# A routed feed-forward kernel: tokens' split forms made one product at a time in a group's last step

## Chip, core and metric

One core of a Trainium2 chip runs the whole program in one launch. The metric is the device time of one execution in microseconds (us); the time before is the median of three runs.

## What is computed

Three stages follow each other: an attention through 32 packed vectors, a dense feed-forward with silu, and a soft mixture of 8 experts with relu. The change lies in the last stage.

```python
def _moe2_ref(x, w_gate, w1, w2):            # x: 2304 x 512, w1: 8 x 512 x 1024, w2: 8 x 1024 x 512
    logits = x @ w_gate
    P = np.exp(logits - logits.max())
    for _ in range(8):
        P /= P.sum(1, keepdims=True) + 1e-09
        P /= P.sum(0, keepdims=True) + 1e-09
        P *= N / E
    for e in range(E):
        h = np.maximum(x @ w1[e], 0.0)
        out += P[:, e:e + 1] * (h @ w2[e])
```

## The kernel before, in words

Every float32 product is made of three matmuls: an operand x is stored as hi (a rounded copy, cast on ACT, line 113) and lo (x - hi, a subtraction on DVE, line 114). The helper `split` issues this pair; such a pair is called a split form below.

The last stage takes the tokens in three groups of two blocks of 384 (`GRP`, line 610), and for each group 16 steps: 8 experts by two halves of the hidden width (`steps`, line 611). A step s multiplies the tokens' 512 channels by a 512 x 512 piece of w1 (`up`, line 822) and, one step later, the hidden values by a piece of w2 (`down` in group 0, `down7` in groups 1 and 2, line 956). Steps 0 to 15 are group 0, 16 to 31 group 1, 32 to 47 group 2.

`up` uses a seven-product scheme on 2 x 2 blocks (two halves of the channels by two blocks of tokens). Its products are numbered 1 to 7 and always run in the order `ORD = [1, 2, 6, 7, 5, 3, 4]` (line 613). Product p multiplies a form of the weights, `wf[s, p]`, by a form of the tokens, `xf[g, c, p]`; c counts the two 128-channel pieces of a half. The token forms of a group are the blocks b11, b21, b22 and four differences: t1 = b12 - b11, t2 = b22 - t1, t3 = b22 - b12, t4 = b21 - t2. They are made once a group and read in all its 16 steps:

```python
        w = wf[s, p]
        for c in range(2):
            x = xf[g, c, p]
            for l, r in ((0, 0), (0, 1), (1, 0)):
                pe.matmul(ps, w[:, l, c, 128 * i:128 * i + 128], x[:, r], ...)
```

`x_forms` (line 747) makes them: first all seven of c = 0, then all seven of c = 1, each a tile [128, 2, 384] in a pool `xf` of 14 slots. So a slot of the next group's form comes free only when the last step of the group has run the product that reads the old one. For group 0 the source is the tokens in SBUF (`pre_forms`, run between the dense stage's tiles); for groups 1 and 2 it is blocks loaded from DRAM by `x_load` (line 1142), 192 KB each, into slots of the pool `cp`, where the differences (`x_tmp`) and the copies of PSUM results in `up` (line 844) also live. That pool has `CP = 10` slots.

The steps are issued by the loop at line 1180. In each step it calls `up` for both row halves i of product n, then a `down` piece, and in between takes a step from a list of background generators (`bg`): loads or forms of the next step's weights, loads of the w2 forms, and last, in a group's last step, `x_forms` of the next group. The list is worked off in order, so what is left of it, `x_forms` above all, is issued by the `while gens` loop after the step's last product.

The order on each engine is not written by hand here: a scheduler turns the calls into one instruction stream per engine, by priority and free slots. All loads and stores go through SP's queue, in order. In groups 1 and 2 the accumulators in PSUM are seeded by ACT (line 969, `d <- M`), and ACT or DVE brings the sums back (lines 981, 983).

## Time and profile before

| what | value |
|---|---|
| median of 3 runs | 1872.11 us (1869.1 to 1873.45) |
| profiled execution, its own time | 1873.27 us |
| its span in the trace | 1871.3 us |
| PE busy | 1835.2 us (98%) |
| DVE busy | 1320.3 us (71%) |
| ACT busy | 931.4 us (50%) |
| attention and dense stage | 0 to about 402 us |
| group 0, 1, 2 | from 401.9, 895.4 and 1370.3 us |

The page cuts the span into 40 slices; PE shows 9 (90% or more) in nearly all of them, with one 8 in slice 30, where the granted clock also shows 8. The start of a group is the start of the first matmul of its first step on PE. Stretches that are named by two times are read from the start of the span.

### The profile page before, as it was taken

The page shows a single profiled execution, that of the slowest core. Times are in us where ns is not written, and L with a number is a line of the kernel's source. Part 1 is how long each engine was busy: PE and PEld are TensorE (multiplying, and loading weights), DVE is VectorE, ACT ScalarE, POOL GpSimd, SP SyncE. Part 2 cuts the span into 40 slices and gives each one's busy share as a digit, 9 for nine tenths or more (in the row PEclk, how much of TensorE's full clock was granted, in tenths as well). Part 3 has the DMA queues.
Part 4 walks back from the last instruction along what each step waited for, and adds up shares of the span by engine and source line. Part 5 has one row for each costly group of instructions (what it writes and reads, how often), then busy time and mean ns, then how long its engine had stood idle before and what let it go on. Part 6 is the DMA issues. An engine that isn't in the chain of part 4 may idle for free.

```text
span 1871.3 us, 28617 instructions
## 1 busy us (share of the span) xinstructions
PE 1835.2 (98%) x10715; PEld 1728.1 (92%) x10715; DVE 1320.3 (71%) x2251; ACT 931.4 (50%) x1842; POOL 2.8 (0%) x10
## 2 busy tenths in 40 slices
PE   6999999999999999999999999999989999999998
PEld 4898999998898989898899999999979999999998
DVE  6877654669987878786666667666677667666676
ACT  5776443444454444443354454545554454444544
POOL 0000000000000000000000000000000000000000
PEclk9999999999999999999999999999989999999999
DMA  9233100088898888887788888888878888888882
GB/s 347 98 90 92 57 13 1 33 294 308 309 335 308 301 304 302 304 306 263 268 259 248 264 259 258 261 251 263 259 226 279 268 259 258 262 247 263 261 255 93
DMA packets 168697, 436.34 MB, mean 233 GB/s; under 512 B 15456, under 2 KB 63216, under 8 KB 168560
## 3 DMA queue, kind: packets, MB, share of 16 engines
q1 hardware_dynamic: 168560, 434.52, 70.4%
q8 instruction: 85, 1.39, 0.3%
q14 instruction: 52, 0.43, 0.1%
HBM read 309.08 MB, written 125.38 MB: 232 GB/s over the span
## 4 chain that ended last, share of the span: by engine, by line
PE 91%; DMA 4%; DVE 2%; ACT 1%; issue 1%; SPq 0%; DVEq 0%; ACTq 0%
PE d L973 25%; PE X L837 21%; PE m L880 13%; PE Z L837 10%; PE g L548 9%; PE Y L837 5%; PE g L514 5%; PE u L490 1%; DMA xr<-x2d 1%; DMA q<-in_qT_dram 1%; DMA rawin<-in_moe_w_in_dram 1%; PE pp L321 0%; PE s L349 0%; PE lg L999 0%; DMA rawout<-in_moe_w_out_dram 0%
## 5 line engine op out<-in xcount | busy, mean ns | idle before, releaser
L973 PE MATMUL d<-hi,w2l 128*128 128x384 f32 x1792 | 495.8, 336 | 0.0
L114 DVE TENSOR_TENSOR lo<-hb,hi 128x768 fp32r<-128x768 f32 x224 | 213.8, 955 | 273.9 <-PE d L973 212.8
L973 PEld LDWEIGHTS d<-hi,w2l 128*128 128x128 f32 x1792 | 327.9, 188 | 6.5 <-ACT d L969 6.5
L973 PE MATMUL d<-lo,w2l 128*128 128x384 f32 x896 | 299.9, 335 | 0.0
L837 PE MATMUL X<-xf,w1l 128*128 128x384 f32 x1536 | 289.3, 336 | 6.3 <-ACT xf L113 5.9
L880 PE MATMUL m<-w2t,h 128*128 128x512 f32 x1152 | 280.4, 393 | 1.2 <-DVE cp L848 1.2
L837 PEld LDWEIGHTS X<-xf,w1l 128*128 128x128 f32 x1536 | 269.2, 189 | 7.9 <-ACT xf L113 6.8
L880 PEld LDWEIGHTS m<-w2t,h 128*128 128x128 f32 x1152 | 214.5, 188 | 43.0 <-DVE cp L848 1.5
L981 ACT COPY M<-d 128x384 f32<-128x384 f32 x232 | 111.7, 481 | 223.7 <-PE d L973 223.7
L113 ACT CAST hi<-hb 128x768 fp32r<-128x768 f32 x224 | 184.0, 836 | 56.6 <-DVE hb L934 30.2
L844 ACT COPY cp<-X 128x384 f32<-128x384 f32 x224 | 107.5, 480 | 207.0 <-PE X L837 207.0
L548 PE MATMUL g<-gT,woh 128*128 128x288 f32 x1024 | 205.7, 296 | 0.0
L548 PEld LDWEIGHTS g<-gT,woh 128*128 128x128 f32 x1024 | 163.6, 188 | 10.5 <-DVE gT L522 6.5
L973 PEld LDWEIGHTS d<-lo,w2l 128*128 128x128 f32 x896 | 168.6, 188 | 0.0
L548 PE MATMUL g<-gT,wol 128*128 128x288 f32 x512 | 150.5, 294 | 0.0
L837 PE MATMUL Z<-xf,w1l 128*128 128x384 f32 x768 | 145.7, 337 | 4.2 <-ACT xf L113 4.2
L837 PE MATMUL X<-xf,wf 128*128 128x384 f32 x768 | 146.7, 338 | 1.8 <-ACT cp L844 1.7
L837 PEld LDWEIGHTS X<-xf,wf 128*128 128x128 f32 x768 | 135.8, 188 | 8.4 <-ACT cp L844 2.9
L837 PEld LDWEIGHTS Z<-xf,w1l 128*128 128x128 f32 x768 | 135.0, 189 | 4.9 <-ACT xf L113 4.5
L983 DVE TENSOR_TENSOR M<-d,M 128x384 f32<-128x384 f32 x204 | 112.3, 551 | 11.7 <-PE d L973 11.6
L969 ACT COPY d<-M 128x384 f32<-128x384 f32 x216 | 104.5, 484 | 18.1 <-DVE hb L810 14.7
L514 PE MATMUL g<-a2h,U 128*128 128x288 f32 x512 | 108.9, 297 | 0.7 <-ACT U L494 0.6
(178 smaller groups left out, 2380.2 us busy)
## 6 DMA issues: line engine op xcount, KB each, us to landing
w1l<-w1d SPq DMA_DIRECT2D x224, 512.0 KB, 4.7
w2l<-w2d SPq DMA_DIRECT2D x224, 512.0 KB, 4.4
w1d<-wf SPq DMA_DIRECT2D x112, 512.0 KB, 5.2
r<-in_moe_w_dram SPq DMA_DIRECT2D x64, 512.0 KB, 5.9
w2d<-T SPq DMA_DIRECT2D x64, 512.0 KB, 4.2
w2d<-w2t SPq DMA_DIRECT2D x96, 256.0 KB, 3.4
rawin<-in_moe_w_in_dram SPq DMA_DIRECT2D x16, 512.0 KB, 4.6
rawout<-in_moe_w_out_dram SPq DMA_DIRECT2D x16, 512.0 KB, 5.5
```

Of the source, the lines that this page charges most:

```text
L113: act.copy(out=hi, in_=raw)
L114: eng.tensor_tensor(out=lo, in0=raw, in1=hi.bitcast(F32), op=ALU.subtract)
L490: pe.matmul(ps[64 * j:64 * j + 64, :w], ppT[b, g][:, 64 * j:64 * j + 64], win[c, k // per][:, k % per, :], start=True, stop=True)
L514: pe.matmul(ps[:, :HS], lhs, rhs, start=(n == 0), stop=(n == 5))
L548: pe.matmul(ps[:, :HS], lhs, rhs, start=(n == 0), stop=(n == 3 * nf - 1))
L837: pe.matmul(ps, w[:, l, c, 128 * i:128 * i + 128], x[:, r], start=(n == 0 and p in ((1, 7) if g else (1, 2, 7))), stop=(n == 5), skip_grou ...
L844: act.copy(out=t, in_=ps)
L880: pe.matmul(ps, h[:, l, 128 * tt:128 * tt + 128], w[:, r], start=(n == 0), stop=(n == 11))
L969: act.copy(out=ps, in_=m)
L973: pe.matmul(ps, w[:, l, c, 128 * d:128 * d + 128], r[:, c], start=(n == 0 and not seed), stop=(n == 5), skip_group_check=seed)
L981: act.copy(out=m, in_=ps)
L983: dve.tensor_tensor(m, ps, m, op=ALU.add)
```

## The change

`x_forms` now works in the order of the products: at each call it makes one form for both channel pieces, in one tile [128, 2, 2, 384], and `xf` is a pool of 7 such slots. For groups 1 and 2 a block of tokens is loaded with both pieces in one transfer of 384 KB into a pool `xr` of 4 slots, which opens when the last step of group 0 begins (where `r1`, the raw w1 pool, is closed). Each cast and each subtraction covers 128 x 768 elements. Differences are written over the block that is no longer read; b22 is overwritten by t2 and loaded a second time for form 3. The generator is no longer in the background list: in a group's last step it is called once after product n, for n from 1 to 6, so that form ORD[n-1] is issued when the product that reads the old one has been issued, and a seventh time after the last. `CP` falls from 10 to 6.

```diff
--- before.py
+++ after.py
@@ -24,7 +24,7 @@
 BLK = 384
 FH = 512
 EPS = 1e-9
-CP = 10
+CP = 6
 
 WID = [512, 512, 512, 512]
 
@@ -744,40 +744,42 @@
         form(3, s4)
         yield
 
-    def x_forms(g, src, tmp):
-
-        for c in range(2):
-            b11, b12, b21, b22 = src(c, 0), src(c, 1), src(2 + c, 0), src(2 + c, 1)
-
-            def form(p, x):
-                t = st["xf"].tile([128, 2, BLK], F32R, tag="xf", name=f"xf{g}{c}{p}")
-                split(t[:, 0], t[:, 1], x)
-                xf[g, c, p] = t
-
-            form(1, b11)
+    def x_forms(g, src, new):
+
+
+        b11, b21, b12, b22 = src(0, 0), src(1, 0), src(0, 1), src(1, 1)
+
+        def less(n, old, a, b):
+            t = new(n, old)
+            for o, x, y in zip(t, a, b):
+                dve.tensor_tensor(o, x, y, op=ALU.subtract)
+            return t
+
+        def form(p, x):
+            t = xf[g, p]
+            for c, y in enumerate(x):
+                c = slice(None) if len(x) == 1 else c
+                split(t[:, 0, c], t[:, 1, c], y)
+
+        def place(p):
+            xf[g, p] = st["xf"].tile([128, 2, 2, BLK], F32R, tag="xf", name=f"xf{g}{p}")
+
+        for n, p in enumerate(ORD):
+            place(p)
+            if p == 6:
+                t1 = less(1, b11, b12, b11)
+                t3 = less(3, b12, b22, b12)
+                t2 = less(2, b22, b22, t1)
+                b22 = src(1, 1)
+                form(6, t2)
+            elif p == 4:
+                form(4, less(4, b21, b21, t2))
+            else:
+                form(p, b11 if p == 1 else b21 if p == 2 else t3 if p == 7 else t1 if p == 5 else b22)
             yield
-            form(2, b21)
-            yield
-            t1, t2 = tmp(g, c, 1), tmp(g, c, 2)
-            dve.tensor_tensor(t1, b12, b11, op=ALU.subtract)
-            dve.tensor_tensor(t2, b22, t1, op=ALU.subtract)
-            form(6, t2)
-            yield
-            t3 = tmp(g, c, 3)
-            dve.tensor_tensor(t3, b22, b12, op=ALU.subtract)
-            form(7, t3)
-            yield
-            form(5, t1)
-            yield
-            form(3, b22)
-            yield
-            t4 = tmp(g, c, 4)
-            dve.tensor_tensor(t4, b21, t2, op=ALU.subtract)
-            form(4, t4)
-            yield
 
     def open_early():
-        st["xf"], s_ = pool("xf", 14, side="right", reuse_waits="tile"); ctx.enter_context(s_)
+        st["xf"], s_ = pool("xf", 7, side="right", reuse_waits="tile"); ctx.enter_context(s_)
         st["r1"], st["r1_st"] = pool("r1", 2, side="right", reuse_waits="tile")
         load_w1(0, 0)
         load_w1(0, 1)
@@ -794,9 +796,13 @@
 
         def src(k, h):
             q = GRP[0][h]
-            return x2[q // 3][k][:, BLK * (q % 3):BLK * (q % 3) + BLK]
-
-        yield from x_forms(0, src, lambda *k: pair(*k)[:, :BLK])
+            return [x2[q // 3][2 * k + c][:, BLK * (q % 3):BLK * (q % 3) + BLK] for c in range(2)]
+
+        def new(n, old):
+            t = unit([128, 2, 512], F32, f"tmpx{n}")
+            return [t[:, c, :BLK] for c in range(2)]
+
+        yield from x_forms(0, src, new)
         yield from w1_forms(0, lambda s, n: pair("w", s, n).rearrange("p (c f) -> p c f", c=2))
 
     X, Y, Z, cp = {}, {}, {}, {}
@@ -832,9 +838,9 @@
         w = wf[s, p]
         n = 0
         for c in range(2):
-            x = xf[g, c, p]
+            x = xf[g, p]
             for l, r in ((0, 0), (0, 1), (1, 0)):
-                pe.matmul(ps, w[:, l, c, 128 * i:128 * i + 128], x[:, r],
+                pe.matmul(ps, w[:, l, c, 128 * i:128 * i + 128], x[:, r, c],
                           start=(n == 0 and p in ((1, 7) if g else (1, 2, 7))), stop=(n == 5),
                           skip_group_check=p in (2, 6, 5, 3, 4))
                 n += 1
@@ -1140,13 +1146,10 @@
         return st["S"].tile([128, 2, 256], F32, tag="S", name=f"S{s}{n}")
 
     def x_load(g, k, h):
-        t = st["cp"].tile([128, BLK], F32, tag="cp", name=f"xr{g}{k}{h}")
+        t = st["xr"].tile([128, 2, BLK], F32, tag="xr", name=f"xr{g}{k}{h}")
         q = GRP[g][h]
-        nc.sync.dma_start(t, x2d[k, :, BLK * q:BLK * q + BLK])
-        return t
-
-    def x_tmp(g, c, n):
-        return st["cp"].tile([128, BLK], F32, tag="cp", name=f"xt{g}{c}{n}")
+        nc.sync.dma_start(t, x2d[2 * k:2 * k + 2, :, BLK * q:BLK * q + BLK].rearrange("k p n -> p k n"))
+        return [t]
 
     load_w2(0, 0)
     load_w2(0, 1)
@@ -1170,7 +1173,6 @@
     def later_pools():
         while old:
             old.pop().close()
-        st["r1_st"].close()
         for name, n, side in (("pb", 2, "left"), ("hb", 6, "left"), ("M", 8, "left"), ("hi", 5, "left"),
                               ("lo", 4, "left")):
             st[name], s_ = pool(name + "2", n, side=side, reuse_waits="tile")
@@ -1188,7 +1190,12 @@
             gens.append(w2_loads(s))
         last_of_group = s < NS and s + 1 < NS and steps[s + 1][0] != steps[s][0]
         if last_of_group:
-            gens.append(x_forms(steps[s + 1][0], lambda k, h: x_load(steps[s + 1][0], k, h), x_tmp))
+            if s + 1 == G0:
+                st["r1_st"].close()
+                st["xr"], s_ = pool("xr", 4, side="right", reuse_waits="tile")
+                ctx.enter_context(s_)
+            xform = x_forms(steps[s + 1][0], lambda k, h: x_load(steps[s + 1][0], k, h),
+                            lambda n, old: old)
         hform = h_forms(s - 1) if s > G0 else iter(())
         next(hform, None)
         for n, p in enumerate(ORD):
@@ -1197,6 +1204,8 @@
                     up(s, i, p)
                     pump_sk()
                     bg()
+                if last_of_group and n:
+                    next(xform)
             if s > G0:
                 next(hform, None)
                 down7(s - 1, DORD[n])
@@ -1214,6 +1223,8 @@
                 bg()
         if G0 <= s < NS and s % 2 == 0:
             load_pb(steps[s][0], steps[s][1] + 1)
+        if last_of_group:
+            next(xform)
         while gens and s < NS:
             bg()
```

What this makes of the streams, at three places. In names, X32, Y32, Z32 are the PSUM tiles of step 32 (a last digit for i), d30 and d31 those of `down7` for steps 30 and 31, xf2cp (before, as xf201: group 2, c = 0, p = 1) and xf2p (now) the token forms, xr the loaded blocks.

PE, where group 2 begins, before:

```order
L837 MATMUL X320_14583<-xf201_14513,w1l32_1_14223 128x384 x3
L837 MATMUL X321_14594<-xf201_14513,w1l32_1_14223 128x384 x3
L837 MATMUL Z320_14707<-xf207_14528,w1l32_7_14305 128x384
L837 MATMUL Z321_14714<-xf207_14528,w1l32_7_14305 128x384
L837 MATMUL Z320_14707<-xf207_14528,w1l32_7_14305 128x384 x2
L837 MATMUL Z321_14714<-xf207_14528,w1l32_7_14305 128x384 x2
L837 MATMUL X320_14583<-xf211_14550,w1l32_1_14223 128x384
L837 MATMUL X321_14594<-xf211_14550,w1l32_1_14223 128x384
L837 MATMUL X320_14583<-xf211_14550,w1l32_1_14223 128x384 x2
L837 MATMUL X321_14594<-xf211_14550,w1l32_1_14223 128x384 x2
L837 MATMUL Y320_14584<-xf202_14516,w1l32_2_14255 128x384 x2
```

PE, the same place now, from the last matmuls of step 31:

```order
L979 MATMUL d3041_14477<-hi30_4_14425,w2l30_4_14165 128x384
L843 MATMUL X320_14501<-xf21_14239,w1l32_1_14180 128x384 x6
L843 MATMUL X321_14512<-xf21_14239,w1l32_1_14180 128x384 x6
L843 MATMUL Y320_14502<-xf22_14283,w1l32_2_14212 128x384 x3
L979 MATMUL d3111_14534<-hi31_1_14497,w2l31_1_14402 128x384
L979 MATMUL d3111_14534<-lo31_1_14498,w2l31_1_14402 128x384
L979 MATMUL d3111_14534<-hi31_1_14497,w2l31_1_14402 128x384
L979 MATMUL d3110_14525<-hi31_1_14497,w2l31_1_14402 128x384
```

Before, products 1 and 7 of the first channel piece stand between those of the second; now product 1 is whole, and `d31` follows after half of product 2.

ACT, the end of step 31, before:

```order
L113 CAST hi31_7_14645<-hb3101_14428 128x768
L113 CAST hi31_5_14684<-hb3100_14263 128x768
L113 CAST xf202_14516<-xr220_14509 128x384
L981 COPY M14_10329<-d3040_14480 128x384
L113 CAST xf206_14523<-xt202_14520 128x384
L113 CAST xf207_14528<-xt203_14526 128x384
L113 CAST xf205_14531<-xt201_14519 128x384
L113 CAST xf203_14534<-xr221_14511 128x384
L113 CAST xf204_14539<-xt204_14537 128x384
L113 CAST xf211_14550<-xr210_14542 128x384
L113 CAST xf212_14553<-xr230_14546 128x384
L113 CAST hi31_6_14724<-hb3111_14385 128x768
```

ACT now, from product 5 of step 31 to the copies of step 32's first product:

```order
L113 CAST xf25_14421<-xr200_14231 128x768
L987 COPY M16_10209<-d3060_14385 128x384
L975 COPY d3020_14429<-M12_10250 128x384
L113 CAST hi31_3_14521<-hb3111_14364 128x768
L113 CAST xf23_14465<-xr211_14329 128x768
L975 COPY d3040_14468<-M14_10286 128x384
L987 COPY M12_10250<-d3020_14429 128x384
L113 CAST hi31_7_14563<-hb3101_14410 128x768
L113 CAST xf24_14487<-xr210_14233 128x768
L987 COPY M14_10286<-d3040_14468 128x384
L113 CAST hi31_5_14602<-hb3100_14220 128x768
L857 COPY Y320_14502<-X320_14501 128x384
```

Before, thirteen of the fourteen casts of group 2's forms stand behind the cast hi31_5, and the last five of them even behind the copies into Y32; now the seven casts stand in step 31, each between seeds (L975) and copies (L987) of `down7`.

SP, in step 31, before:

```order
L1145 DMA xr200_14505<-x2d_111 128x384
L648 DMA w2l31_6_14499<-w2d15_6_9689 128x1024
L1145 DMA xr201_14507<-x2d_111 128x384
L648 DMA w2l31_2_14501<-w2d15_2_9653 128x1024
L1145 DMA xr220_14509<-x2d_111 128x384
L648 DMA w2l31_4_14503<-w2d15_4_9655 128x1024
L1145 DMA xr221_14511<-x2d_111 128x384
L648 DMA w1l33_1_14592<-w1d1_1_4673 128x1024
L648 DMA w1l33_2_14624<-w1d1_2_4687 128x1024
L915 DMA pb21_14881<-pd_110 128x3x128 x2
L1145 DMA xr210_14542<-x2d_111 128x384
```

SP now, where group 1 begins (there is one more load of group 2's tokens, the second of b22, in step 31 behind the second of its w2 loads):

```order
L1151 DMA xr200_14231<-x2d_111 128x2x384
L921 DMA pb10_9892<-pd_110 128x3x128 x2
L921 DMA pb11_10005<-pd_110 128x3x128 x2
L716 DMA w2d15_2_9678<-w2t1510_9675 256x1x256
L716 DMA w2d15_4_9680<-w2t1510_9675 256x1x256
L1151 DMA xr210_14233<-x2d_111 128x2x384
L716 DMA w2d15_2_9678<-w2t1511_9692 256x1x256
L716 DMA w2d15_4_9680<-w2t1511_9692 256x1x256
L1151 DMA xr201_14235<-x2d_111 128x2x384
```

Before, the tokens of group 2 were loaded in step 31 behind the w2 forms; now four of five loads stand at the start of group 1.

## Rows read from the trace of the kernel before

**Rows 1.** Page, part 1: busy time, share of the span and instructions of each engine.

```profile
PE 1835.2 (98%) x10715; PEld 1728.1 (92%) x10715; DVE 1320.3 (71%) x2251; ACT 931.4 (50%) x1842; POOL 2.8 (0%) x10
```

**Rows 2.** Chain in order of time, whole span: start us, us, what.

```profile
882.67 6.48 DMA xr<-x2d
...
1373.36 8.02 DMA xr<-x2d
```

**Rows 3.** Timeline of PE, 868:930: start us, us, engine, line, op; idle before in brackets.

```profile
895.43 0.68 PE L837 MATMUL X<-xf,w1l 128*128 128x384 f32 x3
898.27 1.16 PE L837 MATMUL X<-xf,w1l 128*128 128x384 f32 x5 [2.15 <-ACT xf L113]
899.26 1.20 PE L837 MATMUL Z<-xf,w1l 128*128 128x384 f32 x4
900.88 1.65 PE L837 MATMUL X<-xf,w1l 128*128 128x384 f32 x4 [0.41 <-DVE xf L114]
902.32 0.53 PE L837 MATMUL Z<-xf,w1l 128*128 128x384 f32 x1
902.64 16.67 PE L880 MATMUL m<-w2t,h 128*128 128x512 f32 x72
```

**Rows 4.** Timeline of PE, 1352:1400: the last product of step 31, and step 32.

```profile
1366.12 2.24 PE L837 MATMUL Z<-xf,w1l 128*128 128x384 f32 x12
1368.20 0.33 PE L973 MATMUL d<-hi,w2l 128*128 128x384 f32 x1
...
1370.28 1.21 PE L837 MATMUL X<-xf,w1l 128*128 128x384 f32 x6
1375.67 2.51 PE L837 MATMUL Z<-xf,w1l 128*128 128x384 f32 x6 [4.19 <-ACT xf L113]
1381.97 2.29 PE L837 MATMUL X<-xf,w1l 128*128 128x384 f32 x6 [3.78 <-ACT xf L113]
1384.23 1.01 PE L837 MATMUL Y<-xf,w1l 128*128 128x384 f32 x2
...
1387.99 0.34 PE L973 MATMUL d<-lo,w2l 128*128 128x384 f32 x1
```

**Rows 5.** Groups by shape: busy us, mean ns of one, and idle before.

```profile
L114 DVE TENSOR_TENSOR lo<-hb,hi 128x768 fp32r<-128x768 f32 x224 | 213.8, 955 | 273.9 <-PE d L973 212.8 <-ACT d L969 55.7 <-ACT hi L113 5.3
...
L113 ACT CAST hi<-hb 128x768 fp32r<-128x768 f32 x224 | 184.0, 836 | 56.6 <-DVE hb L934 30.2 <-PE d L973 14.1 <-DVE hb L810 7.6
...
L114 DVE TENSOR_TENSOR xf<-xt,xf 128x384 fp32r<-128x384 f32 x16 | 8.2, 550 | 0.3 <-ACT xf L113 0.2
...
L113 ACT CAST xf<-xt 128x384 fp32r<-128x384 f32 x16 | 7.5, 512 | 4.9 <-DVE xt L763 4.9
```

**Rows 6.** Windows: length, busy PE, PEld, DVE, ACT, POOL (x), PEclk, DMA share, GB/s.

```profile
864.25:895.40 31.15, 31.15 (x157) 28.13 (x156) 20.84 (x37) 13.61 (x28) 0.00 (x0) 1.00 0.82 276
1341.10:1370.28 29.18, 29.18 (x170) 28.95 (x168) 17.95 (x28) 14.63 (x28) 0.00 (x0) 1.00 0.85 275
1370.30:1384.20 13.90, 5.92 (x19) 4.20 (x17) 10.19 (x21) 5.22 (x11) 0.00 (x0) 0.63 0.55 164
402.00:500.00 98.00, 93.54 (x482) 83.49 (x482) 92.22 (x212) 51.97 (x101) 0.00 (x0) 1.00 0.88 315
500.00:531.00 31.00, 31.00 (x157) 27.99 (x156) 28.59 (x51) 15.66 (x31) 0.00 (x0) 1.00 0.91 330
```

**Rows 7.** DMA issues of the whole span: KB each, median us to landing.

```profile
w2l<-w2d SPq DMA_DIRECT2D x224, 512.0 KB, 4.4
...
xr<-x2d SPq DMA_DIRECT2D x16, 192.0 KB, 6.0
```

**Rows 8.** Timeline of SP's DMA queue, 1325:1392: issues of w2 forms in step 31.

```profile
1353.83 6.56 SPq L648 DMA_DIRECT2D w2l<-w2d  x4
```

**Rows 9.** Timeline of ACT, 1340:1390: a form's cast and the seed behind it.

```profile
1365.64 0.51 ACT L113 CAST xf<-xr 128x384 fp32r<-128x384 f32 x1 [3.01 <-DMA xr<-x2d]
1366.06 0.48 ACT L969 COPY d<-M 128x384 f32<-128x384 f32 x1
```

## The prediction

> **What bounds the kernel now.** I read the page's busy times first: PE is busy 1835.2 us of the span, DVE and ACT far less [rows 1]. So only time in which PE waits, or runs slowly, can be won: some 36 us in all. Next I read the chain that ended last, in order of time: between long stretches of matmuls it has a few transfers, and late in the program only loads of token blocks (`xr`), two before each of groups 1 and 2; one of each pair stands here [rows 2]. Then I read PE's timeline around those two places.
>
> Where group 1 begins, PE starts seventeen matmuls of 384 columns between 895.43 and 902.64, waiting twice for token forms [rows 3]. Undisturbed, twelve of them take 2.08 us (1366.12 to 1368.20), 0.173 each [rows 4]. Seventeen would take 2.95, so 7.21 - 2.95 = **4.26 us** are lost.
>
> Where group 2 begins, eighteen such matmuls stand between 1370.28 and 1384.23, with waits of 4.19 and 3.78 us for ACT's casts [rows 4]: 13.95 - 3.12 = **10.83 us**. In this stretch the granted clock averages 0.63, so part of it is spent at the lower level (1.2 GHz instead of 2.4) [rows 6]. The twelve matmuls that follow, from 1384.23 to 1387.99, take 3.76 instead of 2.08 [rows 4]: **1.68 us** more. Together 16.77 us.
>
> The cause is the order of issue. The next group's forms are issued behind everything else of a group's last step, and the second set of loads needs `cp` slots that the first set and its differences hold.
>
> **The change, part by part.**
>
> *Forms between the products.* Product 1 of a new group needs form 1 alone, whose slot comes free when the last step has run product 1, more than 20 us earlier. Form 4, the last, is needed six products into the new group. In PE's new order product 1 of step 32 follows d30_4 with no other form in between. All three lost pieces should go: -16.77 us, the lowered clock with them, since it fell only after PE had waited.
>
> *What the forms cost where they now stand.* Per group ACT gets seven casts of 128 x 768. The same shape takes 0.836 us [rows 5]: 5.9 us, against 14 x 0.512 = 7.2 before. DVE gets seven subtractions for lo, 0.955 each by the same shape [rows 5], and four for the differences; for those I take 0.955 too: 11 x 0.955 = 10.5 us, against 22 x 0.55 = 12.1 before. It is less work, but all of it now falls into the last step. Step 15 (864.25 to 895.40) has DVE busy 20.84 of 31.15 us, of which 8 x 0.55 are already early form work; with 10.5 it becomes 26.9, or 87%. Step 31 (1341.10 to 1370.28) has 17.95 of 29.18, one subtraction of it form work; it becomes 27.9, or 96% [rows 6].
>
> Does PE lose time with DVE so full? Two stretches bound it [rows 6]. From 500 to 531 DVE is busy 28.59 of 31.00 (92%) and PE loses nothing. From 402 to 500 it is busy 92.22 of 98.00 (94%) and PE lacks 4.46 us, 1.4 per 31. So step 15 costs 0 and step 31 between 0 and 1.4; nothing in these steps can be won, since PE is never idle there. I take the middle, 0.7, because DVE's own lateness needs a step to reach PE and step 32 has room again.
>
> *ACT's queue.* A cast that waits holds up the seeds behind it. I followed step 31 product by product: each block of twelve matmuls takes 2.08 us; the cast of a form can start when its old product ends, the seed behind it takes 0.48 [rows 9], and PE needs that seed 4.16 us after the product's end. So 0.836 + 0.48 leaves 2.8 us of room. Cost 0, cover: this room.
>
> *The second load of b22.* It stands in SP's queue behind the second w2 form of step 31. Those forms are issued four in 6.56 us from 1353.83 [rows 8], so its turn comes at about 1356 to 1358. For 384 KB no row exists; 512 KB land in 4.4 us and 192 KB in 6.0 [rows 7], so it lands between 1360 and 1364. Form 3 may be cast when product 3 ends, 2 x 2.08 before 1368.20 [rows 4], at 1364.04. Cost 0; 2.8 us late would still be covered as above, and what is later than that stops PE one for one. It also waits for t4 on DVE, and behind it in SP's queue stand w2 forms that step 32 needs, more than 12 us later. The other loads of group 2 move from step 31 to the start of group 1, into an idle pool.
>
> *CP from 10 to 6.* A step of group 0 takes six `cp` slots (copies 1, 6, 5 for two i) and a later step four, so a slot comes back a step later, when its reader is long done: 0.
>
> *The start of group 0.* The forms of group 0 are made in another order too, on the same number of instructions, and the scheduler shuffles DVE and ACT in steps 0 to 3. This falls into the 98 us in which PE lacks 4.46. Bounds: all of it goes, or it doubles; I take 0.
>
> **Sum.** -16.77 + 0.7 = -16.07. The profiled execution took 1873.27 us, so 1857.2; the median of the runs shown, 1872.11, is 1.16 below it. **Predicted: 1856.0 us.** Bounds of the unknown terms: -4.46 at the start; +4.46, and another 0.7 in step 31: 1851.6 to 1861.2.
>
> **Rivals.**
>
> 1. *The forms hold up ACT and DVE in the last steps: slower.* Each cast waits in ACT's queue for the end of its old product, and behind it stand seeds that PE waits for. For it: before the change a cast held ACT 3.01 us for its data, with a seed behind it [rows 9]. Against: the 2.8 us of room. If cast and subtraction were bare for each of the 14 forms, 14 x (0.836 + 0.955) = 25.1 us would replace 16.77: 1872.1 + 8.3 = 1880. It decides from 16.77 / 14 = 1.2 us a form on. The Trainium skill ("PSUM — Partial Sum Buffer", section "Engine vs sequencer instructions") calls the queues of ScalarE and VectorE strict FIFO; the trace agrees in the 3.01 us just named, and by that rule alone, without the room, the result is this rival's.
> 2. *DVE becomes the bound of both last steps, partly.* At 96% with waits for ACT inside, a lag of a few us reaches PE through late hidden values and undrained banks. For it: 402 to 500. Against: 500 to 531. At 3 to 6 us a step instead of 0.35 on average it takes back 6 to 12: 1861 to 1867.
> 3. *The start of group 0 gets worse.* Steps 0 to 3 run at 94% DVE, and a copy that comes later there is felt. PE lacks up to 4.46 more: 1860.5.
> 4. *The wait only changes its name.* The reloaded block or the weights of step 16 or 32 come next after the forms, and PE stands about as long. For it: loads are on the chain today. Against: SP's order has the weights of the next step ahead of all this. It needs the reload some 17 us later than reckoned; then 1869 to 1874.
>
> **How the numbers follow.** Two runs of this kernel differ by about 0.2%, so 3.7 us is what can be told from no change. My forecast, both waits gone and at most small losses, 1851.6 to 1860: 0.72. Rival 2: 0.10. Rival 3, or both small losses at once, around 1861: 0.07. Rival 4: 0.05. Rival 1: 0.06. Range: from 1851.5 to 1863.5, which takes the forecast, rival 3 and the near part of rival 2 and leaves out somewhat under 0.2. Faster by over 0.2% (below 1868.4): forecast, rivals 2 and 3, 0.89. Within: most of rival 4, 0.05. Slower: rival 1, 0.06.
>
> **What would show it.** Right: no wait of PE for a token form at the two group starts; granted clock 1.00 there; the distance from the start of step 15 to that of step 17, and of 31 to 33, as of any two steps; fourteen casts of 128 x 768 spread over steps 15 and 31; DVE near 96% in step 31. The sum is off if PE has new waits in steps 15, 16, 31 or 32 (for seeds, `hb` or banks), or if the 98 us from 402 change by more than 1 us. It is wrong in kind if PE still waits for `xf`, or if ACT sits for long before a token cast while a seed stands behind it.

## The result and the profile after

The changed kernel takes **1855.02 us**, the median of 4 runs (1853.78 to 1857.59), against 1871.62 of the kernel before, measured beside it (4 runs, 1869.10 to 1873.45). The ratio is 0.9913, 95% interval 0.9901 to 0.9924: faster by 0.9%. Predicted were 1856.0, with a range of 1851.5 to 1863.5. The profiled execution took 1855.88 us, with a span of 1854.1.

Page, part 1, which answers to [rows 1] (busy time, share of the span, instructions of each engine):

```profile
PE 1830.2 (99%) x10715; PEld 1725.7 (93%) x10715; DVE 1317.5 (71%) x2229; ACT 927.7 (50%) x1828; POOL 2.8 (0%) x10
```

PE runs the same 10715 matmuls in 5.0 us less busy time, and the span is 17.2 us shorter: the rest was idle time. PE's timeline at the start of group 1, which answers to [rows 3] (start us, us, engine, line, operation; idle before in brackets):

```profile
892.24 2.92 PE L886 MATMUL m<-w2t,h 128*128 128x512 f32 x12
895.00 2.27 PE L843 MATMUL X<-xf,w1l 128*128 128x384 f32 x12
897.11 0.33 PE L843 MATMUL Y<-xf,w1l 128*128 128x384 f32 x1
897.28 16.52 PE L886 MATMUL m<-w2t,h 128*128 128x512 f32 x72
...
1363.39 0.33 PE L979 MATMUL d<-hi,w2l 128*128 128x384 f32 x1
...
1365.47 2.24 PE L843 MATMUL X<-xf,w1l 128*128 128x384 f32 x12
1367.55 0.68 PE L843 MATMUL Y<-xf,w1l 128*128 128x384 f32 x3
```

The last three rows are the start of group 2, which answers to [rows 4]. At both places twelve matmuls of product 1 run back to back, and no row has a wait. In the list of all waits of PE no token form is left as a releaser. From the start of step 31 to that of step 33 it is 58.63 us, from step 30 to step 32 58.62: the step at the group's start takes no longer than the others.

Windows, which answer to [rows 6] (length; busy PE, PEld, DVE, ACT, POOL with counts; PEclk, DMA share, GB/s): step 15, step 31, step 32 and the first 98 us of group 0.

```profile
863.72:895.00 31.28, 31.28 (x157) 28.22 (x156) 28.57 (x43) 16.22 (x29) 0.00 (x0) 1.00 0.77 275
1336.16:1365.47 29.31, 29.31 (x170) 29.08 (x169) 26.73 (x40) 18.80 (x34) 0.00 (x0) 1.00 0.85 264
1365.47:1395.00 29.53, 29.53 (x171) 29.30 (x171) 22.13 (x35) 13.45 (x26) 0.00 (x0) 1.00 0.89 279
400.46:498.46 98.00, 93.51 (x479) 83.91 (x479) 90.11 (x208) 48.92 (x97) 0.00 (x0) 0.98 0.84 300
```

PE is busy for the whole of steps 15 and 31 although DVE is at 91% in both, and the granted clock where group 2 begins is 1.00 where it averaged 0.63. Neither step is longer than it was; before, steps 15 and 31 began here (the windows of [rows 6] begin 0.10 and 0.13 us later):

```profile
864.15 2.27 PE L837 MATMUL X<-xf,wf 128*128 128x384 f32 x12
...
1340.97 2.24 PE L837 MATMUL X<-xf,w1l 128*128 128x384 f32 x12
```

To the next groups' starts (895.43 and 1370.28) that makes 31.28 and 29.31 us. The groups by shape, which answer to [rows 5], show the forms as they now are (busy us, mean ns of one, idle before):

```profile
L114 DVE TENSOR_TENSOR xf<-xr,xf 128x768 fp32r<-128x768 f32 x14 | 13.3, 952 | 2.4 <-ACT xf L113 2.2
L113 ACT CAST xf<-xr 128x768 fp32r<-128x768 f32 x14 | 11.6, 837 | 4.6 <-DVE xr L755 2.0 <-PE X L843 1.4 <-PE Z L843 0.8
L755 DVE TENSOR_TENSOR xr<-xr,xr 128x768 f32<-128x768 f32 x8 | 7.6, 951 | 0.1
```

ACT's longest wait at a token cast is now 2.0 us, for a difference on DVE, and none is for a load.

The time by stages, for all runs of this study, from the first matmul of steps 0, 16 and 32 and the end of the span:

| run | step 0 starts | group 0 | group 1 | group 2 to end |
|---|---|---|---|---|
| before | 401.9 | 493.5 | 474.9 | 501.0 |
| changed | 400.4 | 494.6 | 470.5 | 488.6 |
| forms at the end | 402.3 | 494.7 | 470.7 | 488.9 |
| early loads alone | 405.5 | 493.1 | 470.7 | 489.0 |
| product order, late loads | 402.8 | 493.1 | 470.7 | 489.2 |
| product order alone | 402.2 | 493.0 | 478.9 | 490.5 |
| halves apart | 401.8 | 493.0 | 470.7 | 488.9 |
| group 0 as before | 400.9 | 494.4 | 470.5 | 488.7 |
| casts x4 | 400.7 | 494.4 | 471.5 | 488.7 |
| subtractions x2 | 402.7 | 495.0 | 470.5 | 488.6 |
| casts x8 | 400.8 | 493.8 | 487.8 | 511.0 |
| subtractions x5 | 403.0 | 493.2 | 480.0 | 499.0 |
| reload x4 | 402.2 | 494.8 | 472.7 | 490.5 |
| balancing spread | 402.9 | 489.6 | 470.7 | 488.9 |

So 4.4 of the 17.2 us went in group 1 and 12.4 in group 2. The first column differs by some 5 us between runs, and by 1.9 between the changed kernel and "forms at the end", whose orders on PE, ACT and DVE are the same up to there: in the second of them PE waits twice for the load of v, which it doesn't in the first, and is 1.4 us behind by 18.8 us. That is the spread of one execution to the next, and so the runs are compared by the columns behind it.

### The profile page after: what moved, and what is told of

It is laid out like the page before. It is cut to its first block, busy times and chain, and to the rows that moved or that the text cites. A ratio compares the mean times of both kernels' runs of the same rounds, so it can differ in the third digit from the quotient of the medians.

```text
span 1854.1 us, 28606 instructions
## 1 busy us (share of the span) xinstructions
PE 1830.2 (99%) x10715; PEld 1725.7 (93%) x10715; DVE 1317.5 (71%) x2229; ACT 927.7 (50%) x1828; POOL 2.8 (0%) x10
## 4 chain that ended last, share of the span: by engine, by line
PE 94%; DVE 2%; DMA 2%; ACT 1%; issue 1%; SPq 0%; DVEq 0%; ACTq 0%
PE d L979 25%; PE X L843 21%; PE m L886 14%; PE g L548 10%; PE Z L843 10%; PE g L514 5%; PE Y L843 5%; PE u L490 1%; DMA q<-in_qT_dram 1%; DMA rawin<-in_moe_w_in_dram 1%; PE pp L321 0%; PE s L349 0%; PE lg L1005 0%; DMA w2d<-w2t 0%; ACT wf L113 0%
## 5 line engine op out<-in xcount | busy, mean ns | idle before, releaser
L979 PE MATMUL d<-hi,w2l 128*128 128x384 f32 x1792 | 495.0, 336 | 0.0
L987 ACT COPY M<-d 128x384 f32<-128x384 f32 x232 | 111.6, 481 | 220.0 <-PE d L979 220.0
L548 PEld LDWEIGHTS g<-gT,woh 128*128 128x128 f32 x1024 | 163.6, 188 | 10.5 <-DVE gT L522 7.3
L989 DVE TENSOR_TENSOR M<-d,M 128x384 f32<-128x384 f32 x204 | 112.3, 550 | 10.9 <-PE d L979 10.7
L975 ACT COPY d<-M 128x384 f32<-128x384 f32 x216 | 104.5, 484 | 18.1 <-DVE hb L816 14.8
```

The costliest lines, as they stand in the source:

```text
L548: pe.matmul(ps[:, :HS], lhs, rhs, start=(n == 0), stop=(n == 3 * nf - 1))
L975: act.copy(out=ps, in_=m)
L979: pe.matmul(ps, w[:, l, c, 128 * d:128 * d + 128], r[:, c], start=(n == 0 and not seed), stop=(n == 5), skip_group_check=seed)
L987: act.copy(out=m, in_=ps)
L989: dve.tensor_tensor(m, ps, m, op=ALU.add)
```

## Experiments

### Which part of the change removes the waits

Four kernels take the change apart. Two of its parts stand against the waits: the tokens are loaded early into a pool of their own, and the forms are made in the order of the products and issued between them.

**Forms at the end.** The call between the products is gone:

```diff
-                if last_of_group and n:
-                    next(xform)
...
-            next(xform)
+            gens.append(xform)
```

> The changed kernel, but the next group's forms stand again in the background list, behind the weights, so that they are issued at the end of a group's last step; the order of the products, the tiles of both channel pieces and the early pool of token blocks stay. Theory A (the prediction's: the place of issue was the cause of the two waits): form 1 comes behind everything of the last step again, PE waits for a token form at both starts and the time is 1862 to 1872. Theory B (the scheduler takes a form forward as soon as its slot and its block are there, so slots and loads were the cause): the same time as the changed kernel within 0.2%, 1852 to 1859, no PE wait for a token form, and the first cast of group 2 early in step 31.

Measured: 1857.95 us (5 runs; ratio 0.9923, 0.9911 to 0.9936). PE starts step 32 at 1367.77, without a gap. ACT's timeline in step 31:

```profile
1341.51 0.84 ACT L113 CAST xf<-xr 128x768 fp32r<-128x768 f32 x1
1345.09 0.84 ACT L113 CAST xf<-xr 128x768 fp32r<-128x768 f32 x1 [0.27 <-PE Y L843]
```

Theory B holds. The first cast of group 2 runs 26 us before the group begins although it is called last, and no wait for a token form is left. Four of group 2's five loads are issued by 904 us, since they have slots of their own. With blocks that are there, the scheduler takes a form forward by itself to where its old product has ended.

**Early loads alone.** From the kernel before, with its fourteen tiles by channel piece and its forms at the end; the loads have the pool of their own and are called when the last step begins:

```diff
-CP = 10
+CP = 6
...
     def x_load(g, k, h):
-        t = st["cp"].tile([128, BLK], F32, tag="cp", name=f"xr{g}{k}{h}")
+        t = st["xr"].tile([128, 2, BLK], F32, tag="xr", name=f"xr{g}{k}{h}")
...
+            xr = {(k, h): x_load(steps[s + 1][0], k, h) for k in range(2) for h in range(2)}
...
```

> The kernel before with one part of the change: the tokens' blocks are loaded whole into a pool of their own (4 slots) that opens when the last step of group 0 begins, three of the differences are written in place and CP is 6; the forms stay in 14 tiles of 128 x 384, all of the first channel piece ahead of those of the second, and are issued at the end of the last step. If late loads were the whole cause: 1853 to 1860, as the change. If the order by channel piece counts as well (the second piece of form 1 needs its old tile, which is free in time, but stands behind six forms of the first piece, the last of which needs the last product of the old group): PE still waits at the start of group 2 for the second piece of product 1, 3 to 7 us at each start in place of 4.3 and 12.5, and the time is 1862 to 1868.

Measured: 1857.94 us (5 runs; 0.9926, 0.9913 to 0.9938), groups 1 and 2 as in the changed kernel within 0.4 us, no wait at either start. The second bound, 3 to 7 us left at each start, did not come: PE's first matmuls of step 32 run without a gap from 1369.31. By the stages early loads alone are the whole gain; the order of the forms and the width of their tiles add nothing to it. The 2.9 us by which its median lies above that of the changed kernel aren't placed: in the profiled execution the difference lies ahead of group 0 (405.5 against 400.4).

**Product order, late loads.** From the changed kernel, with the blocks in pieces of 128 x 384 in the pool of the copies:

```diff
-CP = 6
+CP = 10
...
-        t = st["xr"].tile([128, 2, BLK], F32, tag="xr", name=f"xr{g}{k}{h}")
...
+            t = st["cp"].tile([128, BLK], F32, tag="cp", name=f"xr{g}{2 * k + c}{h}")
...
```

> The changed kernel, but the tokens' blocks come in pieces of 128 x 384 into the pool of the copies (CP 10, no pool of their own), as before, so that they are loaded within the last step; casts and subtractions are of 128 x 384; the forms are issued between the products in their order. If order and place of the forms are what counts: within 0.3% of the changed kernel, 1852 to 1861, because a block has most of a step to come. If the early loads count too: casts stand in ACT's queue waiting for loads with seeds of d behind them, PE waits 2 to 6 us in each last step or at the start of a group, 1861 to 1870.

Measured: 1857.49 us (5 runs; 0.992, 0.9906 to 0.9933), groups 1 and 2 as changed within 0.6 us. SP's timeline shows why: eight of group 2's ten loads are issued 39 to 25 us ahead of the group's start (1366.65), the first five of them with a single load of weights between one and the next.

```profile
1327.49 0.42 SPq L1153 DMA_DIRECT2D xr<-x2d  x1
1329.20 0.32 SPq L648 DMA_DIRECT2D w2l<-w2d  x1
1329.57 0.42 SPq L1153 DMA_DIRECT2D xr<-x2d  x1
...
1339.97 1.37 SPq L1153 DMA_DIRECT2D xr<-x2d  x3
```

ACT's casts in step 31 then wait for PE's old product at most (in step 15 one waits 1.21 us for its load, and no wait of PE follows):

```profile
1340.39 0.93 ACT L113 CAST xf<-xr 128x384 fp32r<-128x384 f32 x2
1360.61 0.93 ACT L113 CAST xf<-xr 128x384 fp32r<-128x384 f32 x2 [1.26 <-PE X L843]
```

So the pool of their own is not needed either, if the call stands between the products: it puts the loads among the weights of the last step in SP's queue, and with ten slots they find room. Whether the same call is enough with the forms still made by channel piece was not tried.

**Product order alone.** As the run before, but with the forms at the end again (the same edit as in the first kernel).

> As the run before this one (blocks in pieces in the pool of the copies, loaded late), but the forms are issued at the end of the last step too: of the change only the order of the products is left. If the order of the forms is nearly all of it: 1853 to 1861. If late loads alone hold PE up: form 1 is the first to be needed and comes no sooner than before, the wait moves from the forms of the second piece to form 1 and stays 4 to 8 us at each start, 1863 to 1872.

Measured: 1864.50 us (5 runs; 0.9962, 0.995 to 0.9975): less than half of the gain, inside the second bound, but not 4 to 8 us at each start. Group 2 loses 1.9 us against the changed kernel, group 1 8.4. SP's timeline in step 31:

```profile
1357.65 6.56 SPq L648 DMA_DIRECT2D w2l<-w2d  x4
1364.30 0.38 SPq L1153 DMA_DIRECT2D xr<-x2d  x1
...
1370.54 5.81 SPq L1153 DMA_DIRECT2D xr<-x2d  x7
```

The loads stand behind the w2 forms and begin 9.8 us ahead of the group's start (1374.10), as they did before. PE at the start of group 1:

```profile
897.33 0.51 PE L843 MATMUL Z<-xf,w1l 128*128 128x384 f32 x2
898.80 0.61 PE L843 MATMUL Z<-xf,w1l 128*128 128x384 f32 x2 [0.95 <-DVE xf L114]
899.25 5.61 PE L886 MATMUL m<-w2t,h 128*128 128x512 f32 x24
908.76 13.94 PE L886 MATMUL m<-w2t,h 128*128 128x512 f32 x48 [3.89 <-DVE acc L908]
```

ACT there:

```profile
904.18 0.51 ACT L113 CAST xf<-xr 128x384 fp32r<-128x384 f32 x1 [5.82 <-DMA xr<-x2d]
```

Product 1 no longer waits, as its form comes first now. But a later form's cast stands 5.82 us in ACT's queue for its load, the subtraction behind it 4.58 in DVE's, and the sums of `m` behind that: PE then waits for a bank, and the 48 matmuls after it take 13.94 us where 72 take 16.52 in the changed kernel; the granted clock averages 0.79 in them. All 28 casts of this kernel's groups 1 and 2 wait 13.0 us for loads. This run and the one before it differ in the place of the call alone, which is worth 10.3 us in groups 1 and 2 here; in a pool of their own ("forms at the end") it is worth nothing. **What decides is when the loads are issued.** In these four runs the place of the call and the pool count as far as they move that.

### How much room the last steps have

The first of these alters the size of the instructions only; the others repeat work whose result is the same.

**Halves apart.** Each cast, subtraction and difference as two of 128 x 384:

```diff
-            for c, y in enumerate(x):
-                c = slice(None) if len(x) == 1 else c
+            for c, y in enumerate(x if len(x) == 2 else [x[0][:, 0], x[0][:, 1]]):
...
```

> The changed kernel, but each cast, subtraction and difference of a form works on 128 x 384 twice, once for each channel piece. By the rows, ACT then gives 14 x 0.512 = 7.2 us to a group's forms in place of 5.9 and DVE 22 x 0.55 = 12.1 in place of 10.5. Theory A (the size of the instructions is covered by the room in the last steps): within 0.2% of the changed kernel, 1852 to 1860. Theory B (the last steps are near the limit of DVE, so 1.6 us more in each are paid): 2 to 4 us longer than the changed kernel, with waits of PE for DVE in step 31 or 32.

Measured: 1856.45 us (5 runs; 0.9918, 0.9905 to 0.993); groups 1 and 2 within 0.3 us. Theory A: the size of the instructions is worth nothing here.

**Casts x4.**

```diff
+                for _ in range(3 if g else 0):
+                    act.copy(out=t[:, 0, c], in_=y)
```

> The changed kernel, but each cast of a token form of groups 1 and 2 is issued four times (the three added write the same tile): 21 x 0.836 = 17.5 us more for ACT in steps 15 and 31, which have 16.2 and 18.8 of 31.3 and 29.3 us busy: 33.8 and 36.3. Theory A (the forms are covered only by ACT's room, and what is over is paid): 2.5 + 7 = 9.5 us at least, partly taken up by steps 16 and 32, so 1857 to 1866, and PE waits for seeds or for token forms in step 31. Theory B (the first rival: each us that holds up ACT's queue is paid by PE): 2 x 17.5 = 35, 1885 to 1890. Theory C (ACT's queue never matters here): as the changed kernel.

Measured: 1858.13 us (5 runs; 0.9925, 0.9912 to 0.9937). The median lies at theory A's low end, but so do those of runs whose stages are as in the changed kernel ("forms at the end", "subtractions x2"); by the stages 1.1 us are lost, and the waits that theory A names in step 31 don't come. So it is near theory C. Steps 15, 31 and 32:

```profile
863.85:895.13 31.28, 31.28 (x158) 28.22 (x156) 26.35 (x41) 27.48 (x46) 0.00 (x0) 1.00 0.71 248
1337.28:1366.59 29.31, 29.31 (x169) 29.00 (x168) 22.44 (x34) 28.36 (x47) 0.00 (x0) 1.00 0.84 267
1366.59:1396.00 29.41, 29.41 (x171) 29.41 (x171) 27.12 (x40) 18.12 (x34) 0.00 (x0) 1.00 0.82 278
```

ACT is at 97% in step 31 and PE still loses nothing in it: casts slip into step 32, where ACT rises from 13.45 to 18.12 us. Groups 1 and 2 together are 1.1 us longer, 1.0 of it in group 1, for 35 us of added casts.

**Casts x8.** The same with seven added.

> As the run with four casts a form, with eight: 49 x 0.836 = 41.0 us more for ACT in steps 15 and 31 each; that makes 57.2 of 31.3 us and 59.8 of 29.3, so 25.9 and 30.5 over. With four casts, 2.5 and 7.0 over, PE lost about 1 us in all. Theory A (what is over is paid, less what the steps behind take up, at least the 9.5 - 1 = 8.5 us seen there): 40 to 48 us lost, 1895 to 1903. Theory B (added work in ACT's queue is paid whole once the queue is behind): 82, 1935 or so. Theory C (the following steps take up far more, since ACT is half idle in them): under 25 lost, below 1880.

Measured: 1895.84 us (4 runs; 1.0127, 1.0112 to 1.0142). Against the changed kernel that is 40.8 us more, for 82 us of casts and 56.4 over the steps' length: theory A, at its low end. The longest of PE's waits is 14.6 us at the start of group 1, for the copies into Y (L859) that stand behind the casts; both such waits, from the list of PE's waits (total us, times, longest us):

```profile
PE Y L845 <- ACT Y L859: 20.7, 2, 14.6
```

A window of step 16:

```profile
894.58:925.00 30.42, 15.18 (x58) 12.30 (x59) 8.90 (x12) 22.18 (x34) 0.00 (x0) 0.72 0.75 250
```

PE is busy for half of it, and the granted clock averages 0.72, after PE has waited. This is what the first rival would look like; four casts a form don't bring it, eight do.

**Subtractions x2.**

```diff
+                if g:
...
+                    for _ in range(1):
+                        dve.tensor_tensor(out=t[:, 1, c], in0=y, in1=t[:, 0, c].bitcast(F32), op=ALU.subtract)
```

> The changed kernel, but each subtraction for lo of a token form of groups 1 and 2 is issued twice: 7 x 0.95 = 6.7 us more for DVE in steps 15 and 31, which have 28.6 and 26.7 of 31.3 and 29.3 busy. At the mean duration that makes 35.2 and 33.4, 4 us over in each. Theory A (DVE is the bound as soon as its sum passes the step): 4 to 8 us longer than the changed kernel, 1859 to 1864, PE waiting for DVE late in step 15 and in step 31 or soon after. Theory B (DVE's lateness is taken up by the buffers and by steps 16 and 32, where it has room): within 2 us of the changed kernel, 1853 to 1858.

Measured: 1858.37 us (5 runs; 0.992, 0.9906 to 0.9934). The medians would allow theory A's least; the stages say B: groups 1 and 2 take 470.5 and 488.6, as in the changed kernel. Steps 15, 31 and 32:

```profile
866.42:897.70 31.28, 31.28 (x158) 28.22 (x156) 30.37 (x46) 16.17 (x29) 0.00 (x0) 1.00 0.67 244
1338.85:1368.16 29.31, 29.31 (x169) 29.08 (x169) 26.80 (x40) 18.20 (x32) 0.00 (x0) 1.00 0.85 264
...
1368.16:1398.00 29.84, 29.84 (x173) 29.61 (x173) 27.30 (x41) 14.02 (x27) 0.00 (x0) 1.00 0.82 265
```

In step 15 DVE is at 97% and PE loses nothing. In step 31 DVE does no more than before (26.80 us); the added work appears in step 32 (27.30 against 22.13).

**Subtractions x5.** The same with four added.

> As the run with each subtraction issued twice, with five: 28 x 0.95 = 26.6 us more for DVE in steps 15 and 31 each: 55.2 of 31.3 us and 53.3 of 29.3, 24 over in each. With twice, 4 over in each, nothing was lost. Theory A (what is over is paid, less the 4 us or more that buffers and the step behind took up there): up to 40 us lost, 1885 to 1897. Theory B (the step behind takes up most of it): 10 to 25 lost, 1865 to 1880.

Measured: 1874.88 us (10 runs; 1.0017, 1.0008 to 1.0027), 19.9 more than the changed kernel, for 53 us of subtractions: theory B. From the list of PE's waits (total us, times, longest us):

```profile
PE d L982 <- DVE lo L114: 5.0, 2, 3.6
PE Z L846 <- DVE cp L870: 4.9, 2, 2.8
```

These are the waits that the second rival named: late hidden values (`lo`) and undrained banks; of the 4.9 us, the smaller wait (2.05) stands in group 0 and in the changed kernel too. In group 1 PE's waits are 8.0 of the 9.5 us lost. In group 2 they are 3.2 of 10.4; there the granted clock averages 0.84 in the first 30 us, with DVE full:

```profile
1376.21:1406.00 29.79, 26.63 (x127) 25.25 (x127) 29.67 (x41) 13.88 (x24) 0.00 (x0) 0.84 0.60 203
```

**Reload x4.** The second load of b22 is issued four times into the same slot:

```diff
+        for _ in range(times):
+            nc.sync.dma_start(t, x2d[2 * k:2 * k + 2, :, BLK * q:BLK * q + BLK].rearrange("k p n -> p k n"))
...
-                b22 = src(1, 1)
+                b22 = src(1, 1, 4) if g else src(1, 1)
...
```

> The changed kernel, but the second load of b22, which form 3 needs, is issued four times into the same slot, each behind the other and behind weights in SP's queue, so that the last lands later by 10 to 20 us. Rival 4 said that a reload some 17 us late would take the place of the waits removed. Theory A (form 3 is needed five products into the new group, some 20 us after its start, and what stands behind its cast in ACT's queue is moved by the scheduler too): within 2 us of the changed kernel, 1853 to 1859, no wait of PE for form 3. Theory B (the cast waits at the head of ACT's queue with seeds behind it, and PE stops one for one beyond 2.8 us): 5 to 15 us at each start, 1865 to 1885.

Measured: 1863.00 us (4 runs; 0.995, 0.9935 to 0.9965), between the theories. ACT, at the start of group 1 and in step 32:

```profile
898.63 0.83 ACT L113 CAST xf<-xr 128x768 fp32r<-128x768 f32 x1 [4.08 <-DMA xr<-x2d]
899.37 0.52 ACT L823 ACTIVATE h<-cp 128x384 fp32r<-128x384 f32 x1
...
1374.60 1.57 ACT L113 CAST xf<-xr 128x768 fp32r<-128x768 f32 x2 [1.72 <-DMA xr<-x2d]
```

PE behind the first of them:

```profile
901.04 0.45 PE L843 MATMUL Y<-xf,w1l 128*128 128x384 f32 x1 [1.73 <-ACT Y L857]
```

Form 3 of group 2 is cast at 1374.60, 4.86 us after the group's start (1369.74); in the changed kernel it was 6.05 before it (1359.42 and 1365.47). So it comes 10.9 us later, and groups 1 and 2 lose 2.2 and 1.8. PE never waits for form 3 itself: it waits for copies and seeds behind the cast. Of the 8.0 us between the medians, these 4.1 and 1.8 of the front are in the profiled execution; the rest isn't placed.

### Group 0

**Group 0 as before.** The changed kernel, with group 0's forms made by channel piece in 128 x 384:

```diff
-        yield from x_forms(0, src, new)
+        for p in ORD:
+            xf[0, p] = st["xf"].tile([128, 2, 2, BLK], F32R, tag="xf", name=f"xf0{p}")
+        for c in range(2):
+            b11, b12, b21, b22 = src(0, 0)[c], src(0, 1)[c], src(1, 0)[c], src(1, 1)[c]
...
```

> The changed kernel, but the forms of group 0 are made as before, all of the first channel piece first, in 128 x 384. In the changed kernel step 0 started 1.5 us sooner and group 0 took 1.1 us longer than before. If the order of group 0's forms does that: step 0 starts again at about 401.9, group 0 takes 493.5, and the time is within 0.5 us of the changed kernel's plus or minus 1.5. If these are shifts of the schedule or of loads at the start of the program: no relation to the order, and the time within 0.2%, 1852 to 1859.

Measured: 1856.51 us (4 runs; 0.9917, 0.9904 to 0.9931). Step 0 starts at 400.9 and group 0 takes 494.4, as in the changed kernel, so the order of these forms isn't the cause of its 1.1 us. "Halves apart", with group 0's code unaltered, has 493.0. What differs is the granted clock, as a window of the changed kernel shows:

```profile
478.00:481.40 3.40, 3.40 (x9) 2.67 (x10) 3.00 (x10) 0.84 (x2) 0.00 (x0) 0.51 0.97 348
```

In these 3.4 us the clock is at its lower level. Six profiled executions have 0.98 over the first 98 us of group 0 (changed, "forms at the end", "group 0 as before", "casts x4", "subtractions x2", "reload x4"), and their group 0 takes 494.3 to 495.0 us. All others have 1.00, and but for "balancing spread" they take 493.0 to 493.8. So the 1.1 us go with the clock of the execution and not with the change; why it falls in some executions and not in "halves apart", where PE has the same three waits in group 0, isn't shown.

**Balancing spread.** PE's 4.5 us in the first 98 of group 0 remain. P's balancing is spread more thinly:

```diff
-        if turn[0] > 16 and turn[0] % 3 == 0:
+        if turn[0] > 4 and turn[0] % 4 == 0:
```

> The changed kernel, with the steps of the balancing of P (its DVE work in the first two steps of group 0) begun earlier and every fourth turn instead of every third. In 400 to 498 the changed kernel's PE lacks 4.5 us, all of it behind DVE or ACT copies, with DVE busy 90.1 of 98. If the density of the balancing makes these waits: 1 to 4.5 us less, 1851 to 1854, PE busy over 95 of the 98. If other DVE work does: the same time within 0.2% and the same three waits.

Measured: 1854.09 us (4 runs; 0.9901, 0.9884 to 0.9917). The window, to be held against the last one of the changed kernel above:

```profile
400.46:498.46 98.00, 95.87 (x512) 85.77 (x507) 91.31 (x213) 50.97 (x101) 0.00 (x0) 1.00 0.87 311
```

The two waits of PE that are left in it:

```profile
431.47 0.39 PE L1045 MATMUL cs<-csum,ones 128*128 128x8 f32 x2 [0.70 <-DVE csum L1042]
438.58 1.32 PE L843 MATMUL X<-xf,wf 128*128 128x384 f32 x6 [1.43 <-ACT cp L850]
```

PE lacks 2.1 instead of 4.5 us and is busy over 95 of the 98, so the density of the balancing made part of these waits. The clock stays at 1.00, and group 0 takes 489.6, the shortest of all runs: 5.0 less than in the changed kernel, of which 2.4 are waits and 2.7 busy time of PE, in part by the lowered clock there (in "halves apart", at full clock, group 0 takes 493.0). By its median it is 0.9 us below the changed kernel, less than can be told.

## Why the prediction was right, and where it was wrong

- **The lost 4.26 us at group 1**: measured 4.38 (474.85 - 470.47). Right.
- **The lost 10.83 + 1.68 = 12.51 at group 2**: measured 12.39 (501.02 - 488.63). The clock's part went with the waits, as reckoned. Right.
- **The cause.** The prediction gave two: the order of issue, with the forms behind everything else of the last step, and loads that need slots which the first set holds. Both are shown, and both act through the loads. With slots of their own the loads come early, and then the place of the call and the order of the forms do nothing ("forms at the end", "early loads alone"): so the place of the forms' own work was not what made PE wait. With the blocks in `cp`, the place of the call is worth 10.3 us ("product order, late loads" against "product order alone"), because it moves the loads in SP's queue; the product order by itself leaves that loss. The sum came out because the change does both things, and either one suffices.
- **DVE in step 31, 27.9 of 29.18 us, cost 0.7**: measured 26.73 of 29.31; step 15 has 28.57 where 26.9 were reckoned. PE loses nothing in either, and both steps are as long as before, 31.28 and 29.31 us. The 0.7 was too much: work that is late passes into the next step, as "subtractions x2" shows, where 6.7 us more still cost nothing.
- **ACT's queue, 2.8 us of room a form, cost 0**: right in its result. Three more casts a form, 2.5 us, lie within this room and cost 0.5 us a group on average; seven more, 5.85 us, are 3.0 over it, and 14 x 3.0 = 42 us stand against 40.8 measured. The size fits, perhaps by chance, since the picture doesn't: PE doesn't stop at each form, casts slip into the next step, and the longest wait stands at the group's start. A cast that *works* can be moved over the step; the scheduler sets the added ones between seeds and copies. A cast that *waits* for a load is what hurts: "product order alone" (5.82 us) and "reload x4" (4.08). The Trainium skill ("PSUM — Partial Sum Buffer", section "Engine vs sequencer instructions") calls these queues strict FIFO; both traces agree, in the 5.82 and 4.08 us at a cast and the work that starts right behind it.
- **The second load of b22**: its turn was reckoned at 1356 to 1358, some 14 to 12 us ahead of group 2's start; it came at 1352.25, 13.2 ahead. Form 3's cast was reckoned 6.2 us ahead of the start and stands 6.05 ahead, behind 1.42 us of waiting for PE, not for the load. Cost 0, right. That beyond 2.8 us each us late stops PE one for one was wrong: 10.9 us late, 8.1 beyond the room, cost 1.8 in group 2.
- **The start of group 0, order 0**: right. PE lacks 4.49 us in the 98 where it lacked 4.46. Group 0 is 1.1 longer, with the lower clock shown above, and the front 1.5 shorter; both are within what executions differ by.
- **CP from 10 to 6, 0**: right as far as stages tell: "early loads alone", with 6, takes 493.1 us for group 0, and "product order, late loads", with 10, the same.
- **The rivals.** 1 (ACT's queue) needs more than four casts a form to show, 2 (DVE) more than two subtractions, 3 did not happen, and 4 is bought at 2 us a group when the reload comes 10.9 us late; its 17 us were not tried.

Against the sum of -16.07 stand 1855.88 - 1873.27 = -17.39 between the profiled executions. Groups 1 and 2 give 4.38 + 12.39 = 16.77 of it, just what was reckoned as lost; 0.43 come from the front and group 0 (895.43 - 895.00) and 0.19 from outside the spans. The term that was mis-sized is the 0.7 for step 31: it is 0. The other 0.62 are chance of one execution, the front's 1.5 us less group 0's 1.1 above all.

## What to carry to other kernels

When PE waits at a group's start for operands that are made from loads, ask first which slot the load waits for: slots of their own for the loads were worth all that reordering the work was. In these runs a queue in order forgave work, even at 97% busy in a step, as long as the next step had room; a head that waited 4 to 6 us for a transfer cost PE time. And a part's worth is only known when it is tried alone: here either of two parts was enough.

## What was not expected of the hardware

The recorded duration of an instruction is longer than its turn in a full queue. DVE in step 31 of the changed kernel:

```profile
1350.37 0.95 DVE L114 TENSOR_TENSOR lo<-hb,hi 128x768 fp32r<-128x768 f32 x1
1351.23 0.95 DVE L755 TENSOR_TENSOR xr<-xr,xr 128x768 f32<-128x768 f32 x1
1352.10 0.95 DVE L114 TENSOR_TENSOR xf<-xr,xf 128x768 fp32r<-128x768 f32 x1
```

Each lasts 0.95 us, but the next starts after 0.86 or 0.87; on ACT, in "casts x4", three casts from 1350.95 take 2.45 us where the mean of one is 0.84. Eleven instructions of 0.955 us are thus 9.6 us of DVE, not 10.5. The Trainium skill ("Perfetto Trace Analysis", section "Optimizing Scalar/DVE Operations") says that the write acknowledgement at the end of an instruction overlaps with the next; the rows agree as to an overlap, of 0.09 us here; that the acknowledgement is what overlaps, no row shows.
